# Attention steps of a recurrent-memory kernel moved from 64-column to 32-column TensorE tiles

## The chip, the cores and the metric

The kernel runs on one core of a Trainium2 chip. The metric is device time in microseconds of one execution; a run of the same kernel was timed three times before the change. A profiled execution of the same kernel gives the trace: start and duration of each instruction on each engine, the waits between engines, and the DMA packets. Engines are named as in the profile: PE is the matrix engine (TensorE), PEld its weight loads, DVE, ACT and POOL the vector, scalar and GpSimd engines, SP the engine whose queue issues most of the DMAs.

## The reference

A gated mix of two branches over one sequence of 2048 tokens with 640 features, all in bf16:

```
out = g * A(x) + (1 - g) * B(x)          g = sigmoid(sum(x * gate_w))
B(x) = (gelu(x @ w_gate) * (x @ w_up)) @ w_down            # 640 -> 1536 -> 640

A:  mem = mem0                                             # 8 rows
    for s in 64 segments of 32 tokens:
        h = [mem ; x_s]                                    # 40 rows
        q, k, v = h @ Wq, h @ Wk, h @ Wv                   # 32 heads of 192
        scores = q @ k.T * 192**-0.5
        scores = where(idx_q < 8 or idx_q >= idx_k, scores, -1e9)
        o = softmax(scores) @ v  ->  @ Wo                  # 40 x 640
        mem = o[:8];  out_s = o[8:]
```

Segment s needs the memory that segment s-1 produced, so the 64 segments run one after another.

## The kernel before

**Stages.** The first part of the program runs the feed-forward branch B and stores it in HBM. Then `segment(s)` runs 64 times. The weights Wq, Wk, Wv, Wo do not fit on the chip all at once: part of them stays, and in each segment about 13 pieces of Wq, Wk and Wv (384 KB each) and 3 of Wo (480 KB each) are loaded over pieces that the segment has used (`load_piece`, L639 to L647, issued by `swap_loads`). One piece, called HALF, is swapped in part only: `HX` bytes of each partition (L563, L642).

**Octets.** The 32 heads are worked in 4 octets of 8 heads. For each octet a segment projects Q, K and V (items "g"), writes the Q and K rows to SBUF (ACT, L1165), turns them with DVE transposes into `Qs` and `Ks` ("tq", "tk", L1179), computes the scores ("sc"), the softmax ("ex"), transposes the probabilities ("pt"), multiplies them with V ("pv") and applies Wo ("wo"). `PROGS` (L517 to L556) lists by hand, for each of four segment kinds, the order of these items on PE. All engines run their own instruction streams in program order, with semaphores between them; a matmul call issues one weight load and one matmul, except `_matmul_kept` (L224), which keeps the weights that are loaded.

**Rows.** 24 of a segment's 32 tokens and the 8 memory rows are computed in the chain ("main", 32 rows, `L`); 8 more rows per segment ("left") are projected ahead for four segments at once, kept in HBM (`qkl`), and copied into `Qs` and `Ks` columns 32 to 40 by `left_fill` on POOL (L1031, L1033). So a score block has R = 40 query and 40 key rows; XA = 24.

**Tiles.** Projections and Wo use four column groups of 32 columns (128x32 tiles), four matmuls side by side. The steps of an octet between them use other tiles. `scores` (L1182): one head pair sits in 3 chunks of 128 rows (192 + 192); the two heads go to column groups 0 and 64 with 40 columns each, first the mask (2 matmuls, L1187), then 8 matmuls over 128 rows (L1195) and 8 over 64 rows (L1200) for the shared middle chunk. `swap` puts the 64-row ones first where a "pv" item follows. `p_transp` (L1239): 4 matmuls for the main part of p (L1245) and 4 for the left part (L1250), in 32-column tiles, both heads in one matmul. `pv_oct` (L1266): for each of 3 chunks and 2 heads a main matmul of 64 columns and 160 moving elements (L1278) and a left one of 64 elements (L1280). The softmax (L1208 to L1237) works on 104 partitions x 160 elements.

**What stands around.** The scores of octet o wait for the transposes of its Q and K (DVE) and for the left rows (POOL); both write buffers that the scores before have read. The p transposes wait for the last softmax step (L1231, L1232 on DVE), the p-V products for the copy of transposed p out of PSUM (L1263 on ACT).

Of the kernel before, what the change touches and what calls it, by code (L numbers as in the profile page):

```python
# [230 lines left out]

def _build(nc, A_x, A_mem0, A_Wq, A_Wk, A_Wv, A_Wo, seg_len, w_gate, w_up, w_down,
# [57 lines left out]
    IP = XA  # L290
    wsA["ident"] = (128 + 2 * IP) * 2
    ST_B = 2 * 3 * 4 * 4 + 8 + 8
    wsA["small"] = al(R * 2 + ST_B)
    wsA["XL"] = al(KT * 32 * 2)
    NVB, NUB = 2, 2
    wsB["K"] = al(12 * R * 2)
# [5 lines left out]
    wsB["p"] = al(4 * 64 * 2)  # L302
# [65 lines left out]
    identp = bview(wsA_off["ident"], (128 + 2 * IP) * 2)  # L368
    ident = identp[:, IP:IP + 128]
    r_ident = sreg(wsA_off["ident"], (128 + 2 * IP) * 2)  # L370
    o_st = wsA_off["small"]
    o_mk = o_st + ST_B
    maskm = bview(o_mk, R * 2)
    r_maskm = sreg(o_mk, R * 2)
# [10 lines left out]
    r_Kl = sreg(wsB_off["K"] + 8, 12 * R * 2 - 8)  # L385
    rows_sb = [bview(wsB_off["rows"] + b * 768, 768) for b in range(2)]
# [6 lines left out]
    pl_sb = bview(wsB_off["p"] + 256, 256).rearrange("p (t k) -> p t k", k=L)  # L393
    r_p = sreg(wsB_off["p"], 512)
    r_pp = [sreg(wsB_off["p"] + 256 * i, 256) for i in range(2)]
# [167 lines left out]
    HX = 384  # L563
# [119 lines left out]
    def load_residents(cls, pick=lambda key: True):  # L683
        for key in first:
# [18 lines left out]
    asel(maskm[:, L:R], r_maskm, [[-1, M]], -L, 1, NEG)  # L703
    asel(maskm[:, L:R], r_maskm, [[0, M]], -L, 1, 0.0)
    asel(maskm[:, L:R], r_maskm, [[0, M]], -XA, 1, NEG)
    for b in (7, 5, 6):
        S_.add("dve", lambda e, b=b: e.memset(ps[:, b, :], 0.0), writes=[r_ps[b]])
# [172 lines left out]
    def ffn_down(blk):  # L880
        n1 = min(Dm, 512)
        for a in range(FA):
# [22 lines left out]
    S_.add("sp", lambda e: e.dma_start(maskm[64:64 + R], maskm[0:R]), reads=[sreg(o_mk, R * 2, 0, 64)],  # L905
           writes=[sreg(o_mk, R * 2, 64, 128)], dma_sem="mask", name="mask copy")
# [4 lines left out]
    for blk in range(NFB):  # L911
# [6 lines left out]
        if blk + 1 < NFB:  # L918
            ffn_transposes(blk + 1)
        else:  # L920
            S_.add("pool", lambda e: e.memset(ident[:, R:64], 0.0), writes=[r_ident])
# [17 lines left out]
    S_.add("pool", lambda e: e.memset(pl_sb, 0.0), writes=[r_p])  # L939
    lb = {}  # L940
# [88 lines left out]
    def left_fill(s, i):  # L1029
# [4 lines left out]
               name="Kl s%d i%d" % (s, i))  # L1034

# [146 lines left out]
    def scores(s, o, swap):  # L1182
        bank = 5 + o % 2
        fns = []
        for gp in (0, 64):
            r0, r1 = (gp, gp + 64) if swap else (0, 128)
            fns.append(lambda e, gp=gp, r0=r0, r1=r1: e.matmul(  # L1187
                ps[gp:gp + R, bank, SC:512].rearrange("p (t r) -> p t r", r=R),
                ident[r0:r1, r0:r0 + R], maskm[r0:r1].rearrange("p (o r) -> p o r", o=1).broadcast_to([r1 - r0, 4, R]),
                start=True, stop=False, tile_position=(r0, gp), skip_group_check=True))  # L1190
        S_.add("pe", fns, reads=[r_ident, r_maskm], writes=[r_ps[bank]], name="mask s%d o%d" % (s, o))
        whole, mid = [], []
        for tl in range(4):
            for gp, c in ((0, 3 * tl), (64, 3 * tl + 2)):
                whole.append(lambda e, gp=gp, c=c, tl=tl: e.matmul(  # L1195
                    ps[gp:gp + R, bank, SC + tl * R:SC + (tl + 1) * R], Qs[:, c, :], Ks[:, c, :], start=False, stop=swap,
                    tile_position=(0, gp), skip_group_check=True))
        for tl in range(4):
            for gp in (0, 64):
                mid.append(lambda e, gp=gp, c=3 * tl + 1, tl=tl: e.matmul(  # L1200
                    ps[gp:gp + R, bank, SC + tl * R:SC + (tl + 1) * R], Qs[gp:gp + 64, c, :], Ks[gp:gp + 64, c, :], start=False,
                    stop=not swap, tile_position=(gp, gp), skip_group_check=True))
        fns = mid + whole if swap else whole + mid
        S_.add("pe", fns, reads=[r_Qm, r_Ql, r_Km, r_Kl], writes=[r_ps[bank]],
# [3 lines left out]
        S3 = ps[0:104, bank, SC:512].rearrange("p (t r) -> p t r", r=R)  # L1208
        mxs = st_f[o % 2][0][0:104, :]
        rst = r_st[o % 2]  # L1210
        mxb = mxs.rearrange("p (t o) -> p t o", o=1).broadcast_to([104, 4, R])
# [6 lines left out]
    def softmax(s, o):  # L1218
        bank = 5 + o % 2
        S3 = ps[0:104, bank, SC:512].rearrange("p (t r) -> p t r", r=R)  # L1220
        mxs, sms, rcs = [x[0:104, :] for x in st_f[o % 2]]
        rst = r_st[o % 2]
        rcb = rcs.rearrange("p (t o) -> p t o", o=1).broadcast_to([104, 4, R])
# [7 lines left out]
        fns = [lambda e: e.tensor_tensor(out=pm_sb[0:104], in0=S3[:, :, 0:L], in1=rcb[:, :, 0:L], op=ALU.mult),  # L1231
               lambda e: e.tensor_tensor(out=pl_sb[0:104, :, M * q:M * q + M], in0=S3[:, :, L:R], in1=rcb[:, :, L:R], op=ALU.mult)]  # L1232
# [6 lines left out]
    def p_transp(s, o):  # L1239
# [4 lines left out]
        for t in range(4):  # L1244
            fns.append(lambda e, t=t: e.matmul(  # L1245
                apx(ps[32 * t:32 * t + 32, bm, R * t:PTW], [[4 * R, 2], [1, R]]), pm_sb[0:104, t, :],
                apx(ident[0:104, 0:128], [[64, 2], [1, R]]), start=True, stop=True, tile_position=(0, 32 * t),
                skip_group_check=True))
        for t in range(4):
            fns.append(lambda e, t=t: e.matmul(  # L1250
                ps[32 * t:32 * t + 32, bank, PTW:PTW + 128].rearrange("p (i b) -> p i b", i=2), pl_sb[0:104, t, :],
                apx(identp[0:104, IP + XA - 16 * t:], [[64, 2], [1, 64]]), start=True, stop=True,
                tile_position=(0, 32 * t), skip_group_check=True))
        if last:
            S_.add("pe", fns[:4], reads=[r_pp[0], r_ident], writes=[r_ps[bm]], name="pT s%d o%d" % (s, o))
            S_.add("pe", fns[4:], reads=[r_pp[1], r_ident], writes=[r_ps[bank]], name="pTl s%d o%d" % (s, o))
# [9 lines left out]
    def pv_oct(s, o):  # L1266
# [7 lines left out]
        def half(c, i):  # L1274
            full = ps[64 * i:64 * i + 64, B if c == 2 else A, W * c:W * c + W]
            part = full.rearrange("p (t r) -> p t r", r=R)[:, :, XA:R]
            e0 = 128 * c + 64 * i
            return [lambda e: e.matmul(full, v[:, e0:e0 + 64], PTm[:, i], start=True, stop=False,  # L1278
                                       tile_position=(0, 64 * i), skip_group_check=True),
# [330 lines left out]
```

## Time and profile before

| | |
|---|---|
| time, median of 3 runs | 1703.07 us (1702.06 to 1715.69) |
| span of the profiled execution | 1701.8 us |
| its own time beside the span | the page gives none |
| DVE busy | 996.0 us (59%) |
| ACT busy | 783.6 us (46%) |
| POOL busy | 251.3 us (15%) |
| moved by DMA | 479.46 MB, mean 282 GB/s |
| first stage (feed-forward, 0 to 188 us) | PE busy 181.68 us |
| 64 segments (188 to 1701.8 us) | PE busy 1386.77 us of 1513.80 us |

How to read the profile: a row of the grouped view gives line, engine, operation, shapes and count, then the busy time, the mean of one in ns, and the idle time of the engine just before. The windows view gives for a stretch of time the busy time of each engine with the number of its instructions behind an x, the granted TensorE clock, the mean busy share of the 16 DMA engines and their rate. The timeline lists instructions in order of time: start, length of the merged group, engine, line, operation, count, and in brackets an idle time of the engine before it with what ended it. "issue" as the end of a wait means that the engine waited for no semaphore and no data that the profile shows. Matmuls side by side overlap, so their mean durations do not add up to busy time.

### The profile page before, as it was taken

What the parts mean: (1) busy time and instruction counts of PE and PEld (TensorE: products, weight loads), DVE (VectorE), ACT (ScalarE), POOL (GpSimd) and SP (SyncE); (2) the same over time, 40 slices, a digit from 0 to 9 for tenths busy, and PEclk for the clock granted to TensorE, in tenths of its full rate; (3) what the DMA queues carried; (4) which work ended last, traced back from release to release, by engine and by line L of the source; (5) the groups of instructions that cost most, each with busy time, mean ns of one, the idle gap of its engine ahead of it and who ended that gap; (6) DMA issues with size and microseconds to landing.
All of it is one profiled execution on the core that took longest, in us unless ns stands there. A gap on an engine that the chain in (4) does not pass through costs nothing.

```text
span 1701.8 us, 79166 instructions
## 1 busy us (share of the span) xinstructions
PE 1568.4 (92%) x39180; PEld 791.4 (47%) x30220; DVE 996.0 (59%) x3256; ACT 783.6 (46%) x1902; POOL 251.3 (15%) x845
## 2 busy tenths in 40 slices
PE   9999889988998999989899989999899999999987
PEld 4554345444444545444544445444444445454444
DVE  2222565666666666656666666656566666666565
ACT  3222454544445454444455444545454454545444
POOL 1100111111111111111111111111111111111111
PEclk9999999999999999999999999999999999999999
DMA  9924888877878788878888788878888787888776
GB/s 318 330 60 146 284 308 296 288 266 279 321 274 284 284 298 306 287 261 290 301 301 299 257 296 293 305 270 285 287 309 315 268 304 280 301 305 307 269 284 253
DMA packets 275928, 479.46 MB, mean 282 GB/s; under 512 B 117862, under 2 KB 144766, under 8 KB 275582
## 3 DMA queue, kind: packets, MB, share of 16 engines
q1 hardware_dynamic: 272526, 471.34, 78.8%
q8 instruction: 271, 4.44, 1.0%
q10 hardware_dynamic: 3056, 3.07, 0.5%
q14 instruction: 75, 0.61, 0.1%
HBM read 453.20 MB, written 21.76 MB: 279 GB/s over the span
## 4 chain that ended last, share of the span: by engine, by line
PE 62%; DMA 21%; DVE 9%; ACT 4%; issue 3%; SPq 0%; DVEq 0%; ACTq 0%
PE ps L226 15%; PE ps L1145 14%; DMA arena<-in_A_Wv_dram 12%; PE ps L1308 10%; DMA left_qk_scratch<-arena 5%; DMA arena<-in_A_Wo_dram 3%; PE ps L872 3%; PE ps L869 3%; PE ps L1278 3%; PE ps L887 2%; PE ps L1333 2%; DVE arena L1319 2%; PE ps L1200 2%; PE ps L956 2%; PE ps L1187 1%
## 5 line engine op out<-in xcount | busy, mean ns | idle before, releaser
L1145 PE MATMUL ps<-arena 128*32 128x384 bf16 x8660 | 653.5, 328 | 42.1 <-DVE arena L1505 22.9
L226 PE MATMUL ps<-arena 128*32 128x384 bf16 x8960 | 633.0, 326 | 5.3 <-DVE arena L1319 3.5
L1145 PEld LDWEIGHTS ps<-arena 128*32 128x32 bf16 x8660 | 226.0, 96 | 404.5 <-issue 261.2
L1179 DVE STREAM_TRANSPOSE arena<-arena 128x384 bf16<-128x384 bf16 x512 | 269.0, 557 | 102.5 <-ACT arena L1165 100.0
L1165 ACT ACTIVATE arena<-ps 128x384 bf16<-128x384 f32 x512 | 229.7, 490 | 195.7 <-PE ps L1145 186.2
L1308 PE MATMUL ps<-arena 128*32 128x320 bf16 x6144 | 271.4, 301 | 8.6 <-issue 7.4
L1308 PEld LDWEIGHTS ps<-arena 128*32 128x32 bf16 x6144 | 170.6, 107 | 64.1 <-issue 15.2
L1168 ACT ACTIVATE arena<-ps 128x384 bf16<-128x384 f32 x256 | 125.3, 489 | 139.9 <-PE ps L1145 132.5
L1292 ACT ACTIVATE arena<-ps 128x384 bf16<-128x384 f32 (+1 forms) x256 | 118.8, 464 | 150.3 <-PE ps L1280 139.3
L1031 POOL COPY arena<-arena 128x96 bf16<-128x96 bf16 x256 | 69.4, 271 | 643.8 <-PE ps L1200 425.8
L1213 DVE TENSOR_REDUCE arena<-ps 104x4 f32<-104x160 f32 x256 | 82.4, 322 | 103.6 <-PE ps L1200 83.2
L1278 PE MATMUL ps<-arena 128*64 128x160 bf16 x1536 | 118.8, 242 | 16.9 <-ACT arena L1263 14.3
L1263 ACT ACTIVATE arena<-ps 128x448 bf16<-128x448 f32 x192 | 104.7, 545 | 64.2 <-PE ps L1250 61.6
L1299 DVE CAST arena<-ps 128x96 bf16<-128x96 f32 (+1 forms) x256 | 63.5, 248 | 96.0 <-ACT arena L1292 43.5
L1278 PEld LDWEIGHTS ps<-arena 128*64 128x64 bf16 x1536 | 80.1, 109 | 84.0 <-ACT arena L1263 34.0
L1227 DVE TENSOR_REDUCE arena<-ps 104x4 f32<-104x160 f32 x256 | 78.5, 306 | 51.4 <-ACT ps L1225 51.2
L956 PE MATMUL ps<-arena 128*32 128x384 bf16 x1280 | 107.4, 328 | 0.0
L1280 PE MATMUL ps<-arena 128*64 128x64 bf16 x1536 | 103.6, 193 | 2.8 <-issue 2.8
L1225 ACT ACTIVATE ps<-ps 104x160 f32<-104x160 f32 x256 | 75.0, 293 | 66.7 <-DVE ps L1215 65.9
L805 POOL COPY arena<-arena 128x120 bf16<-128x120 bf16 x64 | 18.4, 287 | 558.8 <-PE ps L1308 137.8
L963 DVE STREAM_TRANSPOSE arena<-arena 128x384 bf16<-128x384 bf16 x128 | 72.7, 568 | 37.4 <-ACT arena L961 36.7
L961 ACT ACTIVATE arena<-ps 128x384 bf16<-128x384 f32 x128 | 62.4, 491 | 64.6 <-PE ps L956 53.2
(86 smaller groups left out, 1905.3 us busy)
## 6 DMA issues: line engine op xcount, KB each, us to landing
arena<-in_A_Wk_dram SPq DMA_DIRECT2D x335, 384.0 KB, 6.2
arena<-in_A_Wv_dram SPq DMA_DIRECT2D x335, 384.0 KB, 8.4
arena<-in_A_Wo_dram SPq DMA_DIRECT2D x205, 480.0 KB, 6.7
arena<-in_A_Wq_dram SPq DMA_DIRECT2D x146, 384.0 KB, 5.0
arena<-left_qk_scratch SPq DMA_DIRECT2D x126, 96.0 KB, 2.1
left_qk_scratch<-arena SPq DMA_DIRECT2D x49, 192.0 KB, 7.5
arena<-in_A_Wq_dram SPq DMA_DIRECT2D x63, 48.0 KB, 3.2
left_qk_scratch<-arena SPq DMA_DIRECT2D x30, 96.0 KB, 3.9
```

Of the source, the lines that this page charges most:

```text
L226: return e.add_instruction(mybir.InstMatmult(name=nm, start_tensor_calc=like["start"], stop_tensor_calc=stop, tile_size=(128, 32), tile_po ...
L956: fns.append(lambda e, outp=outp, rhs=rhs, j=j: e.matmul(outp, lhs, rhs, start=(k == 0), stop=(k == KT - 1), tile_position=(0, 32 * j)))
L1145: fns.append(lambda e, outp=outp, rhs=rhs, j=j: e.matmul(outp, lhs, rhs, start=(k == 0), stop=(k == KT - 1), tile_position=(0, 32 * j)))
L1165: S_.add("act", lambda e, m=m, bk=bk: e.activation(out=rows_sb[m], in_=ps[:, bk, 0:384], func=ACTF.Copy), reads=[r_ps[bk]], writes=[r_rows ...
L1168: S_.add("act", lambda e, i=i, bk=bk: e.activation(out=v_sb[i % NVB].rearrange("p (c n) -> p c n", c=3), in_=ps[:, bk, 0:384].rearrange("p ...
L1179: S_.add("dve", lambda e: e.transpose(out=dst[:, :, 0:L], in_=rows_sb[m].rearrange("p (c r) -> p c r", r=L)), reads=[r_rows[m]], writes=[r ...
L1213: S_.add("dve", lambda e: e.tensor_reduce(out=mxs, in_=S3, axis=AX.X, op=ALU.max), reads=[rb], writes=[rst], name="smax max")
L1263: S_.add("act", lambda e: e.activation(out=PT, in_=ps[:, bank, 0:PTW + 128], func=ACTF.Copy), reads=[r_ps[bank]], writes=[r_PT], name="pT ...
L1278: return [lambda e: e.matmul(full, v[:, e0:e0 + 64], PTm[:, i], start=True, stop=False, tile_position=(0, 64 * i), skip_group_check=True), ...
L1280: lambda e: e.matmul(part, vl[:, e0:e0 + 64], PTl[:, i], start=False, stop=True, tile_position=(0, 64 * i), skip_group_check=True)]
L1292: S_.add("act", lambda e: e.activation(out=u.rearrange("p t c r -> p c t r")[:, 0:na], in_=pa[:, 0:na, :, 0:L], func=ACTF.Copy), reads=[r_ ...
L1308: fns.append(lambda e, i=i, t=t, j=j, gv=gv: e.matmul(ps[32 * j:32 * j + 32, bank, 0:2 * DJ].rearrange("p (h n) -> p h n", h=2), lhs2[i], ...
```

## The change

- The mask, the scores, the transposes of p and the p-V products all use the 128x32 tiles of the projections.
- Scores: head pair t goes to column group 32t. The 40 query rows of a pair are split into two groups x (24 and 16 rows), and the two heads i are separate column blocks. The mask is 4 matmuls, the scores are 32 (2 passes x 2 row groups x 2 heads x 4 pairs). For the shared middle chunk, head 0 uses the upper 64 rows (`_matmul_upper`); head 1 uses all 128 rows against `KB`, a copy of the lower 64 rows of K with zeros above.
- `KB` is filled by one DVE copy behind each K transpose and one POOL copy behind each left fill.
- The transposes of p are 16 matmuls for the main part and 8 for the left part; the left part of p shrinks to two column blocks.
- The p-V products are 12 main and 12 left matmuls, four column groups each.
- The softmax works on all 128 partitions.
- The mask's copy by DMA and the `swap` order go; four POOL copies build shifted identity blocks at the start.
- `HX` goes from 384 to 960 bytes, since the added buffers take SBUF from the resident weights.

```diff
+def _matmul_upper(e, out, lhsT, rhs, stop, tile_position):
+    nm = e.bass.get_next_instruction_name()
+    return e.add_instruction(mybir.InstMatmult(
+        name=nm, start_tensor_calc=False, stop_tensor_calc=stop, tile_size=(128, 32), tile_position=tile_position,
+        bass_skip_group_check=True,
+        ins=[e.lower_ap(rhs), e.lower_ap(lhsT)], outs=[e.lower_ap(out)]))
...
-    HX = 384
+    HX = 960
...
+    for t_ in range(4):
+        S_.add("pool", lambda e, t_=t_: e.tensor_copy(out=eblk[:, EB * E_AT[t_]:EB * E_AT[t_] + EB], in_=ident[:, 32 * t_:32 * t_ + EB]),
+               reads=[r_ident], writes=[r_ident])
...
-    S_.add("sp", lambda e: e.dma_start(maskm[64:64 + R], maskm[0:R]), reads=[sreg(o_mk, R * 2, 0, 64)],
-           writes=[sreg(o_mk, R * 2, 64, 128)], dma_sem="mask", name="mask copy")
...
+        S_.add("pool", lambda e: e.tensor_copy(out=KB[64:128, :, L:R], in_=sv[64:128, 1].rearrange("p (t c) i -> p t c i", c=3)[:, :, 1]),
+               reads=[rsv], writes=[r_KBl], name="KBl s%d i%d" % (s, i))
...
+        if m:
+            S_.add("dve", lambda e: e.tensor_copy(out=KB[64:128, :, 0:L], in_=Ks.rearrange("p (t c) r -> p t c r", c=3)[64:128, :, 1, 0:L]),
+                   reads=[r_Km], writes=[r_KBm], name="KB s%d o%d" % (s, o))
...
+        S_.add("pe", [lambda e, t=t: e.matmul(
+            ps[32 * t:32 * t + 32, bank, SC:512].rearrange("p (x i r) -> p x i r", x=2, i=2), ident[:, 0:32],
+            maskm.rearrange("p (x o r) -> p x o r", x=2, o=1).broadcast_to([128, 2, 2, R]),
+            start=True, stop=False, tile_position=(0, 32 * t), skip_group_check=True) for t in range(4)],
+            reads=[r_ident, r_maskm], writes=[r_ps[bank]], name="mask s%d o%d" % (s, o))
...
+        for mid in range(2):
+            for x, (q0, q1) in enumerate(((0, XA), (XA, R))):
+                for i in range(2):
+                    for t in range(4):
+                        outp = ps[32 * t:32 * t + q1 - q0, bank, SC + (2 * x + i) * R:SC + (2 * x + i + 1) * R]
+                        c = 3 * t + (1 if mid else 2 * i)
+                        if mid and i == 0:
+                            fns.append(lambda e, outp=outp, c=c, t=t, q0=q0, q1=q1: _matmul_upper(
+                                e, outp, Qs[0:64, c, q0:q1], Ks[0:64, c, :], True, (0, 32 * t)))
+                        else:
+                            rhs = KB[:, t, :] if mid else Ks[:, c, :]
+                            fns.append(lambda e, outp=outp, c=c, t=t, q0=q0, q1=q1, rhs=rhs, mid=mid: e.matmul(
+                                outp, Qs[:, c, q0:q1], rhs, start=False, stop=bool(mid), tile_position=(0, 32 * t),
+                                skip_group_check=True))
...
-        fns = [lambda e: e.tensor_tensor(out=pm_sb[0:104], in0=S3[:, :, 0:L], in1=rcb[:, :, 0:L], op=ALU.mult),
-               lambda e: e.tensor_tensor(out=pl_sb[0:104, :, M * q:M * q + M], in0=S3[:, :, L:R], in1=rcb[:, :, L:R], op=ALU.mult)]
+        fns = [lambda e: e.tensor_tensor(out=pm_sb, in0=S3[:, :, 0:L], in1=rcb[:, :, 0:L], op=ALU.mult),
+               lambda e: e.tensor_tensor(out=pl_sb[:, :, M * q:M * q + M], in0=S3[:, 2:4, L:R], in1=rcb[:, 2:4, L:R], op=ALU.mult)]
...
+        for x, (q0, q1) in enumerate(((0, XA), (XA, R))):
+            for i in range(2):
+                for t in range(4):
+                    c0 = 4 * R * i + R * t
+                    fns.append(lambda e, c0=c0, q0=q0, q1=q1, x=x, i=i, t=t: e.matmul(
+                        ps[32 * t:32 * t + 32, bm, c0 + q0:c0 + q1], pm_sb[:, 2 * x + i, :], ident[:, 32 * t:32 * t + q1 - q0],
+                        start=True, stop=True, tile_position=(0, 32 * t), skip_group_check=True))
+        nm = len(fns)
+        for i in range(2):
+            for t in range(4):
+                fns.append(lambda e, i=i, t=t: e.matmul(
+                    ps[32 * t:32 * t + 32, bank, PTW + 64 * i:PTW + 64 * i + 64], pl_sb[:, i, :],
+                    eblk[:, EB * E_WIN[t]:EB * E_WIN[t] + 64], start=True, stop=True, tile_position=(0, 32 * t),
+                    skip_group_check=True))
...
+        def chunk(c):
+            bk = B if c == 2 else A
+            main, left = [], []
+            for j in range(4):
+                full = ps[32 * j:32 * j + 32, bk, W * c:W * c + W]
+                part = full.rearrange("p (t r) -> p t r", r=R)[:, :, XA:R]
+                e0 = 128 * c + 32 * j
+                main.append(lambda e, full=full, e0=e0, j=j: e.matmul(
+                    full, v[:, e0:e0 + 32], PTm[:, j // 2], start=True, stop=False, tile_position=(0, 32 * j), skip_group_check=True))
+                left.append(lambda e, part=part, e0=e0, j=j: e.matmul(
+                    part, vl[:, e0:e0 + 32], PTl[:, j // 2], start=False, stop=True, tile_position=(0, 32 * j), skip_group_check=True))
+            return main + left
```

More of the change, by code (lines that the diff above doesn't have):

```diff
@@ L392, in _build @@
     pm_sb = bview(wsB_off["p"], 256).rearrange("p (t k) -> p t k", k=L)
-    pl_sb = bview(wsB_off["p"] + 256, 256).rearrange("p (t k) -> p t k", k=L)
-    r_p = sreg(wsB_off["p"], 512)
-    r_pp = [sreg(wsB_off["p"] + 256 * i, 256) for i in range(2)]
+    pl_sb = bview(wsB_off["p"] + 256, 128).rearrange("p (t k) -> p t k", k=L)
+    r_p = sreg(wsB_off["p"], 384)
+    r_pp = [sreg(wsB_off["p"], 256), sreg(wsB_off["p"] + 256, 128)]
     PTW = 8 * R
@@ L1180, in row_transp, with scores @@
                reads=[r_rows[m]], writes=[rd], name="T%s s%d o%d" % ("qk"[m], s, o))
-    def scores(s, o, swap):
+        if m:
+            S_.add("dve", lambda e: e.tensor_copy(out=KB[64:128, :, 0:L], in_=Ks.rearrange("p (t c) r -> p t c r", c=3)[64:128, :, 1, 0:L]),
+                   reads=[r_Km], writes=[r_KBm], name="KB s%d o%d" % (s, o))
+    def scores(s, o):
         bank = 5 + o % 2
-        fns = []
[L1185 to L1204, printed above, removed]
@@ L1272, in pv_oct @@
         W = 4 * R
[L1274 to L1279, printed above, removed]
-                    lambda e: e.matmul(part, vl[:, e0:e0 + 64], PTl[:, i], start=False, stop=True,
-                                       tile_position=(0, 64 * i), skip_group_check=True)]
-        fns = [x for c in range(3) for y in zip(half(c, 0), half(c, 1)) for x in y]
+        def chunk(c):
[10 more added lines that the diff above has]
+            return main + left
+        fns = [x for c in range(3) for x in chunk(c)]
         if s % 4 == 0:
-            S_.add("pe", fns[:2], reads=[r_v[o % NVB], r_PT], writes=[r_ps[A]], name="PV s%d o%d" % (s, o))
-            del fns[:2]
+            S_.add("pe", fns[:4], reads=[r_v[o % NVB], r_PT], writes=[r_ps[A]], name="PV s%d o%d" % (s, o))
+            del fns[:4]
         S_.add("pe", fns, reads=[r_v[o % NVB], r_vl[oc], r_PT], writes=[r_ps[A]] + ([r_ps[B]] if B != A else []), name="PVa s%d o%d" % (s, o))
@@ L1441, in segment @@
             elif kind == "sc":
-                kinds = [it[0] for it in PROGS[q][n - 1:n + 2]]
-                scores(s, i, kinds[2] == "pv" and kinds[0] != "pv")
+                scores(s, i)
                 if i == 0 and q == 0 and g > 0:
```

61 lines of the change are left out of this document (28 added, 33 removed).

## The prediction

> **What bounds the kernel now.** I read the page first: PE is the busiest engine, and a line further down says how its code arrives.
>
> ```profile
> span 1701.8 us, 79166 instructions
> PE 1568.4 (92%) x39180; PEld 791.4 (47%) x30220; DVE 996.0 (59%) x3256; ACT 783.6 (46%) x1902; POOL 251.3 (15%) x845
> q8 instruction: 271, 4.44, 1.0%
> ```
>
> PE ran 39,180 + 30,220 = 69,400 instructions, matmuls and weight loads. Queue q8 brought 271 packets (the first figure; the second is MB) of 4.44 MB / 271 = 16 KB. 69,400 / 271 = 256: one packet is 256 PE instructions. Next the view of the waits, for PE alone:
>
> ```profile
> PE ps L1245 <- DVE arena L1231: 15.5, 33, 0.7
> PE ps L1145 <- DMA arena<-in_A_Wv_dram: 10.3, 26, 0.6
> PE ps L1308 <- issue: 7.4, 15, 0.8
> ```
>
> Three kinds of waits stand side by side: for the softmax, for a piece of weights, and stops behind which nothing stands ("issue"). I looked at the last kind. The timeline has two of them 5.94 us apart; the windows view counts the instructions between such stops (this one and three other pairs); the DMA view of 558.8 to 561.23 us shows the one code packet of that stretch.
>
> ```profile
> 555.29 0.64 PE L1308 MATMUL ps<-arena 128*32 128x320 bf16 x12 [0.43 <-issue]
> 561.23 0.36 PE L1308 MATMUL ps<-arena 128*32 128x320 bf16 x2 [0.32 <-issue]
> q8 instruction: 1, 0.02, 2.3%
> 555.29:561.23 5.94, 4.96 (x128) 3.40 (x128) 2.99 (x11) 2.19 (x5) 0.00 (x0) 1.00 1.04 406
> 1056.93:1062.59 5.66, 4.85 (x128) 3.04 (x128) 3.62 (x14) 3.03 (x7) 0.29 (x1) 1.00 0.86 312
> 844.27:849.39 5.12, 4.55 (x128) 3.76 (x128) 2.22 (x10) 2.09 (x6) 0.48 (x2) 1.00 0.58 224
> 941.59:945.61 4.02, 4.01 (x128) 3.25 (x128) 1.84 (x8) 1.08 (x4) 2.04 (x5) 1.00 0.14 33
> ```
>
> Each stretch holds exactly 128 + 128 = 256 PE instructions: PE stops when one packet is used up and the next has not come. In the first, the packet came only in the last 2.4 us (the DMA view up to 558.8 has none), 3.5 us behind the stretch's start. So one block of code costs at least 5.94 us while the DMA engines are full (share 1.04), 5.66 and 5.12 us at shares of 0.86 and 0.58, and 4.02 us when they are nearly idle (0.14). Beside that limit stands PE's own work, so I looked at one segment of each kind, whole, and then without its first 3 us and its last 3 to 6:
>
> ```profile
> 1041.93:1065.81 23.88, 22.12 (x604) 10.97 (x464) 15.57 (x53) 11.04 (x27) 3.42 (x12) 1.00 0.80 281
> 1065.81:1089.09 23.28, 21.50 (x592) 9.78 (x428) 15.36 (x50) 12.19 (x30) 3.32 (x12) 1.00 0.85 302
> 1089.09:1112.65 23.56, 20.97 (x584) 9.90 (x424) 15.07 (x52) 11.98 (x30) 3.64 (x13) 1.00 0.85 293
> 1112.65:1136.56 23.91, 22.79 (x636) 12.79 (x508) 13.29 (x47) 10.77 (x27) 4.35 (x14) 1.00 0.81 286
> 1044.93:1062.93 18.00, 16.50 (x444) 8.72 (x370) 12.70 (x43) 9.56 (x23) 1.89 (x7) 1.00 0.93 333
> 1068.81:1086.81 18.00, 17.03 (x480) 8.40 (x372) 12.64 (x42) 10.82 (x27) 1.60 (x6) 1.00 0.95 348
> 1092.09:1110.09 18.00, 16.53 (x452) 8.02 (x336) 11.79 (x40) 10.21 (x26) 1.89 (x7) 1.00 0.95 337
> 1115.65:1133.65 18.00, 16.88 (x460) 9.64 (x384) 10.47 (x38) 8.80 (x22) 1.89 (x7) 1.00 0.90 333
> ```
>
> Four segments run 4,240 PE instructions, 1,060 each. The four middles of 18 us hold 3,298, or 825 each: 3.22 blocks, one in 5.6 us, at a DMA share of 0.90 to 0.95. That is hardly slower than the 5.1 to 5.9 us that a block costs there. So in the middle of each segment two limits lie almost on each other: PE's array work, and the delivery of PE's code through DMA engines that are full of weights. Outside the middle there are 235 instructions in 5.7 us, and neither code nor DMA presses.
>
> [...]
>
> **The change part by part.** Array time first. The timeline has one octet's steps between projections (groups of four, 0.16 us apart):
>
> ```profile
> 811.52 0.50 PE L226 MATMUL ps<-arena 128*32 128x384 bf16 x8
> 811.95 0.25 PE L1187 MATMUL ps<-arena 128*40 128x160 bf16 x2
> 812.03 0.26 PE L1195 MATMUL ps<-arena 128*40 128x40 bf16 x8
> 812.23 0.27 PE L1200 MATMUL ps<-arena 64*40 64x40 bf16 x8
> 812.43 0.35 PE L1145 MATMUL ps<-arena 128*32 128x384 bf16 x4
> 812.60 0.34 PE L226 MATMUL ps<-arena 128*32 128x384 bf16 x4
> 812.76 0.21 PE L1245 MATMUL ps<-arena 104*32 104x80 bf16 x4
> 812.80 0.23 PE L1250 MATMUL ps<-arena 104*32 104x128 bf16 x4
> 812.86 0.34 PE L1145 MATMUL ps<-arena 128*32 128x384 bf16 x4
> 813.67 0.34 PE L226 MATMUL ps<-arena 128*32 128x384 bf16 x4
> 813.94 0.26 PE L1278 MATMUL ps<-arena 128*64 128x160 bf16 x2
> 814.03 0.20 PE L1280 MATMUL ps<-arena 128*64 128x64 bf16 x2
> 814.06 0.24 PE L1278 MATMUL ps<-arena 128*64 128x160 bf16 x2
> 814.36 0.35 PE L1145 MATMUL ps<-arena 128*32 128x384 bf16 x4
> ```
>
> Without the other tile sizes the next group would have started at 811.52 + 2 x 0.16 = 811.84. The mask starts at 811.95, so the switch costs 0.11 us, and mask and scores take 0.59 us up to 812.43. The transposes of p (same tiles) take 812.86 - 812.76 = 0.10, p-V 814.36 - 813.83 = 0.53. Together 1.22 us an octet. The new steps have no switch. Their price is per round of four matmuls: a round of 160 elements takes 0.08 (811.95 to 812.03), one of 64 takes 0.03 (814.03 to 814.06). Rounds of 40 elements or fewer I bound by that 0.03 and by the 0.04 of four 80-element ones (812.76 to 812.80), and take 0.03. Mask 1 x 0.08, scores 8 x 0.03, transposes 4 x 0.03 + 2 x 0.03, p-V 3 x (0.08 + 0.03): 0.83 us (0.08 + 0.32 + 0.24 + 0.36 = 1.00 at 0.04). So PE's array saves 0.4 us an octet (0.2 to 0.4), 1.6 us a segment, 102 us in 256 octets if all of it passed.
>
> [...]
>
> Now the code. Matmuls of an octet go from 2 + 16 + 8 + 12 = 38 to 4 + 32 + 24 + 24 = 84, each with a weight load: 92 more PE instructions an octet, 368 a segment (+35%), 23,552 in all, 92 more blocks. Nearly all stand in the middle, which goes to 825 + 368 = 1,193 instructions, 4.66 blocks. PE's own pace there would be 18 - 1.6 = 16.4 us, 3.5 us a block, less than any block above has cost. So delivery decides. A middle begins within a block, and the block behind it is mostly there; three or four more must come. I take three, at 5.66, 5.12 and 4.02 us (the share falls when the stage stretches past the loads), 14.8 us, and 1.66 blocks at PE's own 3.5 us, 5.8 us: 20.6 us instead of 18, +2.6 us a segment. The lower end has all three at 4.02 us: 17.9 us, no change. The upper end has four blocks at all four rows, 20.7 us, and 0.66 x 3.5 = 2.3 us: 23.0, +5.0. I stay midway: the middle's share of 0.90 to 0.95 belongs to the slow rows, and the spreading of the same loads over a longer stage to the quick ones. 64 x 2.6 = 166 us.
>
> Other edits:
>
> ```profile
> L1232 DVE TENSOR_TENSOR arena<-ps,arena 104x32 bf16<-104x32 f32 x256 | 46.2, 181 | 0.0
> arena<-in_A_Wq_dram SPq DMA_DIRECT2D x63, 48.0 KB, 3.2
> ```
>
> - The DVE copy into KB costs about L1232's 0.18 us, 256 times, and stands between the K transpose and the scores; the next transposes and softmax steps queue behind it. I cost it at nothing, as PE comes later to those waits; without that cover it is up to 0.18 x 256 = 46 us. The POOL copy costs no more, on an engine that is busy 15% of the time; PE's cover hides it too.
> - HX adds 72 KB to each of 63 loads: at the 281 to 302 GB/s of a segment 0.25 us of DMA. I cost it at nothing, as the DMA engines are nearly idle at a segment's end (share 0.14 in the row above); with that gone it is 64 x 0.25 = 16 us.
> - Softmax rows go from 104 to 128 partitions with as many elements each: nothing. The smaller left part of p gains at most half of L1232, 23 us of DVE, off PE's path. The start's POOL copies cost under 1 us; the mask's DMA goes.
>
> The sum is made against the span: 1701.8 + 166 = 1868 us. The median of the runs is 1.3 us above the span, so I predict 1869 us. The forecast's own range is from +0.8 us a segment (1753) to +4.4 (1983).
>
> **The rivals.** *Code stays hidden, and the array saving shows (faster).* [...] Against it: exactly 256 instructions between the stops. Not all of 102 us would pass: PE already waits for weights in front of L1145 (26 times), and pieces do not land sooner because PE is early. With the first half of each segment given back to them, 51 us remain: 1652 us. [...]
>
> *The softmax chain takes the saving (no change).* PE waits for L1231 at 33 of 256 octets already. KB lengthens the chain by 0.18 us an octet, 0.7 us a segment; half of the array's 1.6 us passes, 0.8. The two cancel: 1703 us, or 1686 to 1720.
>
> **How the numbers follow.** About 1% is what a measurement of this kernel can tell from no change. Forecast 0.79, faster rival 0.15, no change 0.06; that gives slower 0.79, same 0.06, faster 0.15. The range leaves out the faster rival and the last of the upper end: 1690 to 1985 us.
>
> **What would show it.** In the profile after: near 363 code packets in q8; PE instructions up to about 51,000 + 42,000; far more idle time of PE with "issue" behind it, in front of scores, transposes and p-V, in the middle of segments; 256 instructions between two such stops; gaps of 0.1 us between projections and scores gone. DVE's and ACT's waits for PE grow. I am wrong if blocks of 256 pass in under 4 us at DMA shares above 0.9, or if PE's idle time has the softmax or the weights behind it.

## The result and the profile after

The kernel after takes 2009.6 us (median of 4 runs, 2002.8 to 2020.3) against 1705.7 us for the kernel before on the same chip: 1.179 times the time, 95% interval 1.173 to 1.185. The prediction was 1869 us with a range up to 1985. The direction and the cause hold, the size does not: the forecast was 2.6 us more per segment, and (2002.4 - 1701.8) / 64 = 4.7 us came. The page of the kernel after, with the lines that answer to those of before:

```profile
span 2002.4 us, 103103 instructions
...
PE 1584.3 (79%) x50937; PEld 886.2 (44%) x41996; DVE 1057.8 (53%) x3512; ACT 787.6 (39%) x1902; POOL 304.1 (15%) x1105
...
q8 instruction: 363, 5.95, 1.2%
...
PE 64%; issue 17%; DVE 13%; ACT 5%; DMA 0%; POOL 0%; SPq 0%; DVEq 0%; ACTq 0%; POOLq 0%
```

PE has more instructions and nearly the same busy time, so it idles 21% of the span instead of 8% (418 us instead of 133; why the busy time did not fall comes with the clock, further down). The 363 packets are the 271 of before and the 92 forecast, and 363 x 256 = 92,928 is the count of PE's instructions within a few (50,937 + 41,996 = 92,933). The last line is the chain that ended last; in the kernel before it reads

```profile
PE 62%; DMA 21%; DVE 9%; ACT 4%; issue 3%; SPq 0%; DVEq 0%; ACTq 0%
```

The share of DMA is gone (the page's next line there gives 12% to loads of Wv, 3% to loads of Wo and 5% to the transfer of left rows to HBM), and "issue", time in which PE waited for nothing that the profile shows, has gone from 3% to 17%. The waits of PE in the kernel after (total, times, longest):

```profile
PE ps L1160 <- issue: 60.0, 30, 3.3
PE ps L1334 <- issue: 37.3, 27, 3.5
PE ps L1219 <- issue: 37.3, 23, 4.4
PE ps L1305 <- issue: 35.9, 15, 3.2
PE ps L1303 <- issue: 33.0, 18, 2.9
PE ps L1266 <- issue: 32.7, 18, 2.8
PE ps L1272 <- issue: 23.4, 12, 3.2
PE ps L1160 <- DVE arena L1530: 23.1, 35, 1.2
```

The seven longest entries all have "issue" behind them; the first of another kind comes eighth. They stand in front of projections (L1160; L1145 in the old file), Wo (L1334), scores (L1219), p-V (L1303, L1305) and transposes of p (L1266, L1272). All of the view's "issue" entries for PE add up to 309 us in 181 stops; in the kernel before they are 23 us in 42 stops, and its 19 us of waits for weights are gone. Counted over the whole trace, each of the 180 intervals from one stop to the next holds a whole multiple of 256 PE instructions, to within 2: PE stops where a block of code ran out. But it does not stop at every block: 100 of the intervals hold one block, the other 80 hold two to five.

The windows view shows what a block costs now. Each of these stretches holds one block and ends in a stop; the first three also begin at one (columns as before; the last two are DMA share and GB/s):

```profile
1205.47:1211.96 6.49, 3.83 (x138) 2.30 (x119) 4.07 (x14) 1.89 (x5) 1.48 (x6) 1.00 1.04 396
1211.96:1217.35 5.39, 2.94 (x128) 2.06 (x129) 2.27 (x8) 2.27 (x5) 0.00 (x0) 1.00 0.83 281
1158.36:1163.20 4.84, 3.14 (x134) 2.33 (x122) 2.94 (x10) 2.10 (x5) 0.00 (x0) 1.00 0.74 233
1191.25:1195.00 3.75, 3.38 (x131) 2.92 (x129) 1.37 (x6) 1.50 (x5) 1.96 (x5) 1.00 0.11 31
```

Each stretch has 256 PE instructions again (up to four more, where a group of four straddles an edge). PE needs 2.9 to 3.8 us for them and gets them every 6.49 us at a DMA share of 1.04, down to every 3.75 us at 0.11. In four segments, from 3 us behind the start on, for 21 us:

```profile
1116.08:1137.13 21.05, 16.38 (x620) 9.02 (x512) 12.70 (x42) 10.18 (x25) 2.50 (x10) 0.92 0.81 294
1143.08:1164.08 21.00, 15.20 (x550) 8.28 (x437) 12.24 (x40) 8.39 (x22) 2.21 (x9) 0.92 0.86 293
1172.05:1193.05 21.00, 17.03 (x643) 10.64 (x568) 11.32 (x41) 8.90 (x22) 3.38 (x12) 0.92 0.81 289
1199.39:1220.39 21.00, 15.05 (x560) 8.56 (x488) 12.38 (x43) 8.75 (x21) 2.50 (x10) 0.93 0.83 292
```

That is 2,373 + 2,005 = 4,378 instructions in 84 us: a block of 256 each 4.9 us on average. Nine stops lie in these 17 blocks. Between them PE passes some blocks without a stop, but not quickly; here are four blocks, across the start of a segment at 1169.05, with a stop of 2.50 us at their end alone:

```profile
1163.20:1182.42 19.22, 14.76 (x572) 7.64 (x451) 12.11 (x42) 9.06 (x23) 4.29 (x16) 1.00 0.77 267
```

Over all segments, the 180 blocks that end in a stop take 5.4 us each on average, and the 169 others between the first and the last stop 4.9 us.

### The profile page after: what moved, and what is told of

Read it like the earlier page. It is cut to its first block, busy times and chain, and to the rows that moved or that the text cites. A ratio compares the mean times of both kernels' runs of the same rounds, so it can differ in the third digit from the quotient of the medians.

```text
span 2002.4 us, 103103 instructions
## 1 busy us (share of the span) xinstructions
PE 1584.3 (79%) x50937; PEld 886.2 (44%) x41996; DVE 1057.8 (53%) x3512; ACT 787.6 (39%) x1902; POOL 304.1 (15%) x1105
## 4 chain that ended last, share of the span: by engine, by line
PE 64%; issue 17%; DVE 13%; ACT 5%; DMA 0%; POOL 0%; SPq 0%; DVEq 0%; ACTq 0%; POOLq 0%
PE ps L1160 15%; PE ps L226 13%; PE ps L1334 11%; DVE arena L1194 4%; PE ps L1219 3%; PE ps L1303 3%; PE ps L888 3%; PE ps L885 2%; PE ps L1359 2%; PE ps L903 2%; PE ps L1266 2%; PE ps L969 2%; ACT arena L1318 2%; DVE arena L1345 1%; ACT arena L1285 1%
## 5 line engine op out<-in xcount | busy, mean ns | idle before, releaser
L1160 PE MATMUL ps<-arena 128*32 128x384 bf16 x8660 | 699.6, 343 | 83.5 <-issue 60.0
L226 PE MATMUL ps<-arena 128*32 128x384 bf16 x8960 | 655.3, 331 | 21.6 <-issue 14.3
L1160 PEld LDWEIGHTS ps<-arena 128*32 128x32 bf16 x8660 | 260.2, 100 | 436.8 <-issue 337.2
L1194 DVE STREAM_TRANSPOSE arena<-arena 128x384 bf16<-128x384 bf16 x512 | 275.8, 562 | 126.5 <-ACT arena L1180 123.4
L1334 PE MATMUL ps<-arena 128*32 128x320 bf16 x6144 | 305.5, 322 | 41.0 <-issue 37.3
L1180 ACT ACTIVATE arena<-ps 128x384 bf16<-128x384 f32 x512 | 229.7, 490 | 255.4 <-PE ps L1160 244.7
L1334 PEld LDWEIGHTS ps<-arena 128*32 128x32 bf16 x6144 | 197.7, 113 | 97.6 <-issue 50.4
L1183 ACT ACTIVATE arena<-ps 128x384 bf16<-128x384 f32 x256 | 125.3, 490 | 174.7 <-PE ps L1160 168.3
L1303 PE MATMUL ps<-arena 128*32 128x160 bf16 x3072 | 133.5, 245 | 50.0 <-issue 33.0
L1231 DVE TENSOR_REDUCE arena<-ps 128x4 f32<-128x160 f32 x256 | 82.2, 321 | 142.3 <-PE ps L1219 137.5
L1219 PE MATMUL ps<-arena 128*24 128x40 bf16 (+1 forms) x6144 | 111.3, 183 | 52.8 <-issue 37.3
L1305 PE MATMUL ps<-arena 128*32 128x64 bf16 x3072 | 121.6, 201 | 36.0 <-issue 35.9
L1303 PEld LDWEIGHTS ps<-arena 128*32 128x32 bf16 x3072 | 93.0, 101 | 91.6 <-issue 40.1
L1245 DVE TENSOR_REDUCE arena<-ps 128x4 f32<-128x160 f32 x256 | 81.8, 319 | 88.9 <-ACT ps L1243 86.0
L1219 PEld LDWEIGHTS ps<-arena 128*16 128x16 bf16 (+1 forms) x6144 | 89.5, 91 | 84.7 <-issue 39.5
L969 PE MATMUL ps<-arena 128*32 128x384 bf16 x1280 | 118.1, 347 | 6.3 <-issue 6.3
L1266 PE MATMUL ps<-arena 128*32 128x16 bf16 (+1 forms) x4096 | 78.7, 175 | 53.5 <-issue 32.7
L1266 PEld LDWEIGHTS ps<-arena 128*32 128x32 bf16 x4096 | 72.3, 99 | 100.2 <-issue 38.3
```

The lines of the kernel that those rows point to most:

```text
L226: return e.add_instruction(mybir.InstMatmult(name=nm, start_tensor_calc=like["start"], stop_tensor_calc=stop, tile_size=(128, 32), tile_po ...
L969: fns.append(lambda e, outp=outp, rhs=rhs, j=j: e.matmul(outp, lhs, rhs, start=(k == 0), stop=(k == KT - 1), tile_position=(0, 32 * j)))
L1160: fns.append(lambda e, outp=outp, rhs=rhs, j=j: e.matmul(outp, lhs, rhs, start=(k == 0), stop=(k == KT - 1), tile_position=(0, 32 * j)))
L1180: S_.add("act", lambda e, m=m, bk=bk: e.activation(out=rows_sb[m], in_=ps[:, bk, 0:384], func=ACTF.Copy), reads=[r_ps[bk]], writes=[r_rows ...
L1183: S_.add("act", lambda e, i=i, bk=bk: e.activation(out=v_sb[i % NVB].rearrange("p (c n) -> p c n", c=3), in_=ps[:, bk, 0:384].rearrange("p ...
L1219: fns.append(lambda e, outp=outp, c=c, t=t, q0=q0, q1=q1, rhs=rhs, mid=mid: e.matmul(outp, Qs[:, c, q0:q1], rhs, start=False, stop=bool(mi ...
```

## The experiments

**Only the number of instructions.** Small matmuls were added to the kernel before, nothing else of the change: `pads` goes in front of the mask, the transposes of p and the p-V products.

```diff
+    def pads(bank, c, n):
+        return [lambda e, j=j % 4: e.matmul(ps[32 * j:32 * j + 32, bank, c:c + 4], ident[:, 0:32], ident[:, 0:4], start=True,
+                                            stop=True, tile_position=(0, 32 * j), skip_group_check=True) for j in range(n)]
...
-        S_.add("pe", fns, reads=[r_ident, r_maskm], writes=[r_ps[bank]], name="mask s%d o%d" % (s, o))
+        S_.add("pe", pads(bank, PTW, 18) + fns, reads=[r_ident, r_maskm], writes=[r_ps[bank]], name="mask s%d o%d" % (s, o))
```

> The kernel before, its own tiles and products, with 46 small matmuls of 4 columns, each with its own 32-column weight load, added in every octet: 18 in front of the mask, 16 in front of the transposes of p, 12 in front of the P-V products. That is 92 PE instructions per octet, the number that the change adds, and no other part of the change. Their array time is 11.5 rounds of at most 0.04 us, so at most 118 us in all. Theory code (PE's instructions arrive too slowly): 363 packets on the instruction queue as after, PE stops ahead of score, transpose and P-V products again with no engine behind them, clock below 0.98, and 1950 to 2110 us. Rival (the new tiles, the copy of K or the bytes of the change cost the time, not the count of instructions): at most 1703 + 118 = 1821 us, and stops of at most 60 us in all.

> The same with half as many added matmuls (9, 8 and 6; 46 PE instructions per octet, 46 packets more, 317 in all). Theory code: between the two, and less than half of the way if the first blocks still fit under the work: 1760 to 1880 us. Rival: at most 1703 + 59 = 1762 us.

Measured, one run each beside 1713.4 us for the kernel before: 2001.6 us with all 46, 1852.2 us with half. From the page of the run with all 46, then from its waits of PE, then from the windows view:

```profile
PE 1727.5 (86%) x50956; PEld 987.1 (49%) x41996; DVE 1005.0 (50%) x3256; ACT 787.7 (39%) x1902; POOL 252.5 (13%) x845
...
q8 instruction: 363, 5.95, 1.2%
```

```profile
PE ps L1183 <- issue: 58.4, 43, 2.8
PE ps L1145 <- issue: 34.6, 24, 2.4
PE ps L1314 <- issue: 29.5, 22, 2.6
```

```profile
1222.10:1228.04 5.94, 3.09 (x128) 2.31 (x128) 1.98 (x7) 2.27 (x5) 0.00 (x0) 0.99 1.00 374
```

The last row is one block between two stops: 128 + 128 instructions, 3.09 us of PE's work, 5.94 us at a DMA share of 1.00. None of the new tiles, no copy of K and no larger `HX` is in this kernel, and it has the time of the kernel after within 8 us. That it comes so near is in part chance: its stops add up to 197 us, not 309, and PE is busy 159 us longer than in the kernel before (1727.5 against 1568.4), some of it at a lower clock (mean 0.955). The next run separates the packets from the matmuls. The price is the same from the first block on: (1852.2 - 1713.4) / 46 = 3.0 us for each of the first 46 packets, (2001.6 - 1852.2) / 46 = 3.2 us for each of the next. The bound of 1821 us for array time alone is passed by 180 us.

**As many matmuls, fewer instructions.** The same 46 matmuls, but 34 of them issued without a weight load (`ldweights=False`):

```diff
+        return [lambda e, j=j: (first if j < 4 else kept)(e, j % 4) for j in range(n)]
```

> The kernel before with the same 46 added small matmuls per octet, but only the first four at each of the three places load their weights (12 loads); the other 34 keep them. So 58 PE instructions per octet more instead of 92, 58 packets, 329 in all, at the same number of matmuls. Theory code: 58 x 3.0 to 3.25 us = 174 to 189 us, so 1870 to 1900 us. Rival (the added matmuls cost it, each by itself): about 2000 us as with all 46 loads.

Measured 1889.3 us against 1706.6 us, ratio 1.106 (1.102 to 1.110): 182.7 us for 58 packets, 3.15 us each. Against all 46 with loads (288.2 us for 92 packets) that is 105.5 us less for 34 packets, 3.1 us each again, at the same number of matmuls. The price follows the packets, not the matmuls.

**Array time instead of instructions.**

```diff
+        wide = lambda e: e.matmul(ps[0:32, A, 0:448], ident[:, 0:32], PT[:, 0:448], start=True, stop=True,
+                                  tile_position=(0, 0), skip_group_check=True)
```

> The kernel before with as much added array time as the 46 small matmuls had at most, but in two instructions per octet instead of 46: one matmul of 160 columns ahead of the mask and one of 448 columns ahead of the P-V products, on one 128x32 tile each, both overwritten by the products that follow. By the 128x160 and 128x384 rows (245 and 328 ns) that is 0.4 to 0.6 us per octet, 100 to 150 us in all, with 4 packets more on the instruction queue. Theory code: 1780 to 1860 us, with next to no stops, since array time costs itself at most and four instructions per octet nothing. Rival (added array time costs more than itself, and the 46 small ones were dear for that): 1950 us or more.

Measured 1732.7 us against 1704.8 us (one run): +28 us, less than either theory said.

```profile
PE 1635.8 (95%) x39692; PEld 836.0 (48%) x30732; DVE 997.7 (58%) x3256; ACT 783.2 (45%) x1902; POOL 252.5 (15%) x845
...
q8 instruction: 275, 4.51, 1.0%
```

PE is busy 1635.8 - 1568.4 = 67 us longer, and 28 us of that reach the end. The array work that was added is smaller than I worked out from the rows (67 us, not 100 to 150), and more than half of it fits into PE's waits. So 67 us of array work cost 28 us, and the array work of 46 small matmuls, 118 us at most by my estimate, cost 288 us with its loads.

**Without the weights beside it.** The products run on whatever lies in the buffers; the weight loads inside the segments are left out.

```diff
-            load_piece(other, "swap s%d" % seg)
+            loaded[slot_id[other]] = other
```

> The kernel after without the weight loads inside the segments: the products run on the weights that lie in the buffers, so half of the swapped weights are the wrong ones, and nothing else changes. PE's instructions are the same 93,000. Theory code: what slows a block is that its packet shares the DMA engines with the weights, and a block on nearly idle DMA engines took 4.02 us before; stops fall from about 310 us to under 100, the clock rises above 0.98, and the time is 1650 to 1800 us. Rival (array, copy of K, softmax chain): the weights are not what the after waits for, so 1950 us or more.

> The kernel before without the weight loads inside the segments (half of the swapped weights are the wrong ones). The control for the run above. Theory code: the waits for weights go and nothing takes their place, 1560 to 1690 us, and the two kernels without the loads lie within 100 us of each other. Rival: the two without the loads lie as far apart as with them, some 300 us.

Measured: 1651.1 us for the kernel after and 1633.0 us for the kernel before without these loads (one run each). The time of the kernel after falls by 2009.6 - 1651.1 = 358 us (the 2009.6 us are the median of the first section), that of the kernel before by 80 us (from 1713.4 us, on the same chip). From the page, the waits and the windows of the kernel after without the loads:

```profile
PE 1495.3 (91%) x50956; PEld 835.6 (51%) x41996; DVE 1048.8 (64%) x3512; ACT 785.7 (48%) x1902; POOL 303.9 (18%) x1105
...
q8 instruction: 363, 5.95, 1.6%
```

```profile
PE ps L1266 <- DVE arena L1249: 24.3, 41, 0.8
...
PE ps L1219 <- DVE arena L1197: 19.3, 48, 1.4
...
PE ps L1359 <- issue: 5.3, 11, 0.8
```

```profile
1150.90:1154.65 3.75, 3.25 (x136) 1.86 (x120) 2.63 (x9) 2.10 (x5) 0.14 (x1) 1.00 0.02 4
1154.65:1158.12 3.47, 3.02 (x128) 2.12 (x128) 2.17 (x8) 1.89 (x5) 0.29 (x1) 1.00 0.18 38
```

The 363 packets are the same, but the longest stop entry is 5.3 us and all of them together are 25 us. What is left between two stops is 3.47 and 3.75 us for a block at DMA shares of 0.18 and 0.02. So it is the weight loads beside it that make a block dear (6.49 us at a share of 1.04 in the kernel after), and with the DMA engines nearly idle a block that PE must wait for still cost these 3.47 and 3.75 us. Whether code and weights meet in the DMA engines or in HBM was not tried.

**The copy of K.** The two copies are left out, and the products that read `KB` read K.

```diff
-            S_.add("dve", lambda e: e.tensor_copy(out=KB[64:128, :, 0:L], in_=Ks.rearrange("p (t c) r -> p t c r", c=3)[64:128, :, 1, 0:L]),
...
-                            rhs = KB[:, t, :] if mid else Ks[:, c, :]
+                            rhs = Ks[:, c, :]
```

> The kernel after without the zero-padded copy of K: neither the DVE copy (256 of 192 ns) nor the POOL copy (256 of 208 ns) is made, and the four products that used it read K itself, so those scores are summed over both halves of the rows. PE's instructions stay as many. Theory code: the code sets the pace, the copies lie beside it: 1990 to 2020 us, within 1% of after. Rival (the copies stand in the chain to the softmax): 2009 - 256 x 0.19 = 1960 us or less.

> The same, and without the weight loads inside the segments (1651 us with the copies). With the loads gone PE waited for DVE in 23% of the chain, against 10% without the change. Theory code: the copies do cost once the code no longer hides them: 1600 to 1640 us. If the copies cost nothing here either, 1645 to 1655 us.

Measured: 2006.5 us (2001.1 to 2029.3), ratio to the kernel before 1.182 (1.174 to 1.191), against 1.179 for the kernel after: no difference. Without the weight loads as well 1625.1 us, 26 us below the 1651.1 with the copies (one run each), and PE's wait for the K side in front of the scores falls from the 19.3 us above to

```profile
PE ps L1214 <- DVE arena L1192: 7.0, 15, 1.1
```

The copies lie beside the code stops, as forecast, and would cost up to 26 us if those went. This last figure compares two single runs on two chips, on which the kernel before took 1713.4 and 1704.8 us.

**The larger split load.**

```diff
-    HX = 384
+    HX = 960
```

> The kernel before with only the size of the one split load changed, 960 bytes per partition instead of 384 (74 KB more in each segment). Theory code: 1695 to 1720 us, no difference that can be told. Rival (bytes): the added bytes take 74 KB at some 300 GB/s, 0.25 us per segment, 16 us in all: 1715 to 1730 us.

Measured 1718.5 us (1706.6 to 1721.5), ratio 1.0067 (1.0031 to 1.0102): about 11 us, near the bytes' 16 us and not nothing. PE's wait for pieces of Wv, 10.3 us before, is

```profile
PE ps L1145 <- DMA arena<-in_A_Wv_dram: 16.8, 33, 1.0
```

**One part alone, one part undone.** p-V in 32-column tiles in the kernel before, and p-V in 64-column tiles in the kernel after; each takes the other file's lines of `pv_oct`:

```diff
-        fns = [x for c in range(3) for y in zip(half(c, 0), half(c, 1)) for x in y]
+        fns = [x for c in range(3) for x in chunk(c)]
```

> The kernel before with only the p-V part of the change: 24 matmuls on 128x32 tiles instead of 12 on 128x64 ones, so 24 PE instructions per octet more, 24 packets, 295 in all. Array time of p-V falls from 0.53 us per octet to the 0.29 us that the timeline of after shows where it ran without a stop, 61 us in all. Theory code, at the 3.0 to 3.3 us that a packet more cost in the runs with added small matmuls: +72 to +79 us, less at most part of the saving: 1750 to 1790 us. Rival (array time decides): 1640 to 1705 us.

> The kernel after with only the p-V part undone (12 matmuls on 128x64 tiles, 24 packets fewer, 339 in all). Theory code: 24 x 3.1 = 75 us back, the array's 0.24 us per octet hidden: 1915 to 1960 us. Rival (array time decides): 2009 us or more.

Measured: p-V alone 1767.2 us against 1704.9 us, ratio 1.037 (1.032 to 1.042), 2.6 us for each of 24 packets, the array's saving included; "issue" entries of 100 us instead of 23. The kernel after with p-V undone 1938.9 us, 71 us less than the kernel after. Both are where the count of packets puts them, and p-V, whose array time falls by 0.24 us an octet (0.53 to 0.29) where no stop interferes, is a loss by itself.

**The same instructions at another place.** 92 small matmuls per segment in one row, ahead of the last products of Wo. They write into the bank that holds the sums of those products, which changes these sums.

```diff
+            if item[2] == 1:
+                S_.add("pe", [lambda e, j=j % 4: e.matmul(
+                    ps[32 * j:32 * j + 32, OB2, PTW:PTW + 4], ident[:, 0:32], ident[:, 0:4], start=True, stop=True,
+                    tile_position=(0, 32 * j), skip_group_check=True) for j in range(92)],
+                    reads=[r_ident], writes=[r_ps[OB2]], name="pads s%d" % s)
```

> The kernel before with the same number of added small matmuls as the run with half of them (92 per segment, 46 packets in all), but all together at the end of each segment, ahead of its last Wo products, where the DMA engines are nearly idle and PE's 235 instructions take 5.7 us. Theory code with the price of a packet set by the weights beside it: 235 + 184 instructions are 1.64 blocks, 6.1 us at the 3.75 us of a block on nearly idle DMA engines, so +0.4 us, or the added array time of 0.9 us, a segment: 1730 to 1770 us. If a packet costs 3 us wherever it stands: 1850 us.

Measured 1830.4 us (1828.9 to 1841.0), ratio 1.076 (1.069 to 1.082): 125.5 / 46 = 2.7 us a packet, far above my 1730 to 1770 and near the other case, 3 us wherever a packet stands. The end of a segment in the timeline (start, length, line, count, and in brackets the idle time before):

```profile
1054.94 0.59 PE L1338 MATMUL ps<-arena 128*32 128x160 bf16 x24
1055.35 0.58 PE L1332 MATMUL ps<-arena 128*32 128x4 bf16 x52
1057.05 0.43 PE L1332 MATMUL ps<-arena 128*32 128x4 bf16 x40 [1.12 <-issue]
```

And the windows view from one stop to the next:

```profile
1053.03:1057.05 4.02, 2.90 (x128) 2.27 (x128) 1.88 (x6) 1.22 (x4) 1.16 (x3) 1.00 0.42 123
```

That is one block, 4.02 us at a share of 0.42. My expectation spread the instructions evenly over the stage. In fact the last Wo products and the added matmuls are short, PE runs through 76 matmuls in the 1.0 us from 1054.94 to 1055.93, and then stands. So DMA engines that are more than half idle (share 0.42) did not make this place cheap: PE ran out of instructions there 1.12 us before the next block was in.

## Why the prediction was right in its cause and too low in its size

- *Code delivery takes the place of the array as the bound.* Right, and shown: the same number of PE instructions without the rest of the change gives 2001.6 us, fewer weight loads at the same number of matmuls cost less in step with the packets, and without the weights on the DMA engines the 309 us of stops shrink to 25. It does not bind at every block: about half of them pass without a stop.
- *The number of blocks, 92 more, 363 in all.* Right.
- *The price of one block.* Right as a range: 5.94 to 4.02 us by DMA share in the prediction's rows, 6.49 to 3.75 us in the kernel after. The share alone does not fix it: of 131 blocks at shares above 0.9, six passed in under 4 us, which I had named as a sign of being wrong.
- *What the blocks of a segment cost.* This is the step that failed: "I take three, at 5.66, 5.12 and 4.02 us (the share falls when the stage stretches past the loads), 14.8 us, and 1.66 blocks at PE's own 3.5 us, 5.8 us". That the block behind a middle's start is mostly there was my estimate, which no run shows by itself; the count of paid blocks that came of it was about right: 181 stops in 64 segments are 2.8 each. Both prices were too low. A block that ends in a stop takes 5.4 us on average, not 14.8 / 3 = 4.9, so the paid ones are 2.83 x 5.42 = 15.3 us. A segment of the kernel after takes (2002.4 - 188) / 64 = 28.35 us, so 13.0 us are left for the blocks without a stop, where I had 5.8 us in the middle and the 5.7 us outside it, 11.5 us. By the count above they take 4.9 us each on average, in the middle and outside it, well above PE's own 3.5. This is the larger part of the 2.1 us a segment that my 2.6 us lack. The runs with added matmuls agree: already the first 46 packets cost 3.0 us each, so none of the added blocks was free. The measured +4.7 us lies under my own upper end of +5.0, which I had cut to +4.4 for the forecast's own range.
- *The clock, for which the prediction has no term.* With the same instructions, PE is busy 1584.3 us in the kernel after and 1495.3 us without the weight loads, where the stops are down from 309 to 25 us and the mean granted clock is 0.998 instead of 0.951: 89 us, or 1.4 us a segment, of longer array work. Much of it lies in the blocks without a stop (mean clock 0.93 in them). How much of it reaches the end, and what else holds these blocks back, stays open.
- *Array saving of 0.4 us an octet (0.83 us instead of 1.22).* Right where no stop interferes, and nothing of it is left in the time. In the kernel after:

```profile
1144.44 0.50 PE L226 MATMUL ps<-arena 128*32 128x384 bf16 x8
1144.77 0.24 PE L1202 MATMUL ps<-arena 128*32 128x160 bf16 x4
1144.84 0.27 PE L1219 MATMUL ps<-arena 128*24 128x40 bf16 x16
...
1145.06 0.36 PE L1160 MATMUL ps<-arena 128*32 128x384 bf16 x4
...
1213.57 0.24 PE L1303 MATMUL ps<-arena 128*32 128x160 bf16 x4
...
1213.86 0.58 PE L1334 MATMUL ps<-arena 128*32 128x320 bf16 x12
1214.27 0.26 PE L1266 MATMUL ps<-arena 128*32 128x24 bf16 x16
1214.43 0.24 PE L1202 MATMUL ps<-arena 128*32 128x160 bf16 x4
```

  Mask and scores take 0.29 us from their start to the next projection, p-V 0.29 and the transposes 0.16: 0.74 us. The mask follows the two projection groups ahead of it (1144.44 + 2 x 0.16 = 1144.76) without the 0.11 us by which the mask comes later than that in the kernel before. Even with the weight loads and the copies of K left out, the kernel with the change reaches 1625 us against 1633 us, 8 us of a possible 0.48 x 256 = 123. By the pages of these two runs PE's busy time falls by 1538.4 - 1486.8 = 52 us there, and its idle time grows by 44 us, 29 of them code stops. Why the busy time falls by 52 and not by 123 was not settled; the 0.48 us come from single octets.
- *KB at nothing.* Right under the cover of the code stops; 26 us of the 46 us bound appear without it.
- *HX at nothing.* Wrong by some 11 us, 0.2 us a segment, in the kernel before. What it adds to the kernel after was not measured.
- *The rivals.* "Code stays hidden" falls with the stops, and it would not have been the gain that I gave it: with the weights away, both kernels stand at 1651 and 1633 us. The softmax chain as the bound falls with the run without the copies of K, and with the added matmuls, which leave the chain as it was and cost as much.

## What to carry to other kernels

Count instructions beside array time. Here PE ran 256 instructions in 2.9 to 3.8 us between two stops, and the next 256 took 3.5 to 6.5 us to arrive, by what else was on the DMA engines; in that state the split into more and smaller matmuls cost the delivery of its code, whatever the array gained: the span grew by 301 us. Stops of PE with nothing behind them, a whole multiple of 256 PE instructions apart, were the sign, and the kernel before, with only 42 of them (23 us), had no reserve: the first 46 packets added to it cost 3.0 us each. So where such stops show, price every added block. With the weight loads running, each packet that more and smaller matmuls brought cost 2.6 to 3.3 us here, the change itself included, wherever its instructions stood. Array work added there moved the end by less than itself (67 us of it cost 28 us), so fewer instructions are what to look for; with kept weights, 34 packets fewer made 105 us of difference.

## What the runs showed of the hardware that was not expected

Delivery was slow even with the DMA engines nearly idle: 3.75 and 3.47 us for a block of 256 instructions at DMA shares of 0.02 and 0.18, in the kernel after without the weight loads. Nor did the crossing from block to block stay hidden behind PE's work: the kernel after shows 181 stops, 309 us in all, the kernel before 42 and 23 us.

The granted clock (1 is full speed) fell with the stops, from a mean of 0.997 in the kernel before (23 us of stops) to 0.951 in the kernel after (309 us); it was 0.978 with half of the added matmuls (122 us), 0.955 with all of them (197 us), and 0.998 for the kernel after without the weight loads (25 us). A stretch behind a stop of the kernel after, in the timeline and in the windows view:

```profile
1131.79 0.20 PE L234 MATMUL ps<-arena 64*16 64x40 bf16 x4 [2.11 <-issue]
...
1132.21 0.53 PE L1160 MATMUL ps<-arena 128*32 128x384 bf16 x4
```

```profile
1132.05:1135.46 3.41, 3.41 (x124) 2.03 (x104) 2.31 (x9) 2.35 (x6) 0.00 (x0) 0.50 0.28 95
```

PE comes out of a stop of 2.11 us at 1131.79, and for the 3.41 us from 1132.05 on the clock is 0.50; four projection matmuls take 0.53 us instead of the 0.34 to 0.36 elsewhere. How much of the lost time is due to such stretches was not tried. A bound can be estimated: a mean of 0.951 over 2002.4 us is 98 us of full clock withheld, of the 301 us by which the span grew. It fits the 89 us of longer busy time above, which hide what the array work lost. In the run with kept weights the mean is 0.983, 32 us withheld of 1888, and the packets still cost 183 us.
